# Two layers of sliding-window attention and MLP: a list scheduler's order, q and k projected token-major and transposed by DMA

## The chip, the core and the metric

The kernel runs on one core of a Trainium2 chip. The metric is the device time of one launch in microseconds (us). Engines are named PE (TensorE), ACT (ScalarE), DVE (VectorE), POOL (GpSimd) and SP (SyncE, which here only issues DMAs). Each engine works through its own list of instructions in order and waits on semaphores for the others.

## What is computed

Sequence 2048, width D = 576, 32 heads of 18, a causal window of 256, MLP width F = 4608. Two layers with the same weights, each an attention block and an MLP block with residuals:

```python
def _A_ref(x, wqkv, wo):            # H = 32, Dh = 18, W = 256
    qkv = (x @ wqkv).reshape(B, S, 3, H, Dh)...
    scores = einsum("bhqd,bhkd->bhqk", q, k) * Dh ** -0.5
    mask = (i - j >= 0) & (i - j < W)
    p = softmax(where(mask, scores, -1e9))
    return einsum("bhqk,bhkd->bhqd", p, v)... @ wo
def _B_ref(x, w1, b1, w2, b2):
    y = _layernorm(x)
    return gelu(y @ w1 + b1) @ w2 + b2
x = x + _A_ref(_layernorm(x), wqkv, wo)
x = x + _B_ref(_layernorm(x), w1, b1, w2, b2)   # and both once more
```

Inputs and output are bfloat16.

## The kernel before

**Tiles and chunks.** The sequence is 16 tiles of 128 tokens; four tiles make a chunk, so two layers are eight chunks (`NK`). x stays in SBUF as float32 (`x_res`). Everything for a chunk k: layer norm (`ln_stats` on DVE at L280 and L282, `ln_rstd` on ACT as exp of a logarithm at L286 and L288, the normalise on DVE at L299), a transpose by DMA from SP (L302) to `xnTa` or `xnTm`; projections to q, k, v; attention; out-projection; layer norm again; MLP.

**Projections.** `qk_piece` (L329) computes q and k feature-major: the stationary operand is a slice of weights spread to 32 columns per head (`wq_pad`, `wk_pad`, built at the start by `scat`), the moving one is `xnTa` with 512 token columns; five matmuls for four heads, evicted at L335 or L337 directly into `qT` and `kT`. `v_piece` (L356) is token-major: `xnTa` stationary, 288 columns of `wv_sb` moving. `kT` is a ring of six tiles, `vA` one of ten; `qT` has one buffer.

**Attention.** Eight groups of four heads, three units each. `scores` (L388) writes PSUM banks 0 to 3, ACT takes the exponentials into `pT` (L396, two instructions), POOL masks (L407), `pv` (L426) accumulates in bank 4, DVE divides into `attq`. `att_T` transposes `attq` by DMA (L446), `outproj` (L464) and `resid` (L454) add to x.

**MLP.** In two halves of 18 slices of F. `mm1` (L479): five matmuls of 512 columns per slice into banks 0 to 3, gelu on ACT into `hT` (L483; one buffer for both halves). `mm2_piece` (L491): 288-column matmuls over the slices into banks 5 and 6, then `resid`. Weights are loaded by DMA from SP for every chunk anew (`w1_load` L309, `w2_load` L316). At L666 POOL adds the bias b2 to x.

**Order.** `Sched` (L36 on) records a list per engine in the order of the calls and inserts waits. The order is written by hand in the loop at L614. Iteration k, with km = k - 1: normalise for chunk k+1; `G_part(km, 0)` is mm1 of the first half; `E_part(k, 0)` is heads 0 to 3 of chunk k with mm2 of that half and q and k pieces of chunk k+1 as fillers between the units; `G_part(km, 1)`; `E_part(k, 1)` with the second half's mm2; then the tail: `att_T`, the last q and k pieces, `outproj` with statistics and normalise to `xnTm`, v pieces and the last mm2 tile between, and the w2 loads. The next iteration begins with mm1, which reads that `xnTm`. Iteration 8 has only the MLP of the last chunk. ACT loads the gelu table before and the exp table after each `G_part`.

Of the kernel before, what the change touches and what calls it, by code (L numbers as in the profile page):

```python
# [7 lines left out]
P = 128  # L8
# [148 lines left out]

def build_kernel(nc, A_x, A_wqkv, A_wo, B_x, B_w1, B_b1, B_w2, B_b2, out):
    S_ = 2048
# [5 lines left out]
    G = 8  # L165
    NT = S_ // P
# [5 lines left out]
    DHALF = 288  # L172
    CT = 4
    NCH = NT // CT
    CW = CT * P
    NK = NL * NCH
# [4 lines left out]
    NB1 = 4  # L181

    S = Sched(nc)

# [4 lines left out]
    w1_sb = sb("w1_sb", [P, NB1, KD, 512], BF16)  # L189
# [5 lines left out]
    xnTa = sb("xnTa", [P, KD, CW], BF16)  # L195
    xnTm = sb("xnTm", [P, KD, CW], BF16)
    qT = sb("qT", [P, G, CW], BF16)
# [3 lines left out]
    attq = sb("attq", [P, CT, KD * 128], BF16)  # L201
    attT = sb("attT", [P, KD, CW], BF16)
    hT = sb("hT", [P, NFH, 512], BF16)
    NXN = 4
# [5 lines left out]
    lnv = sb("lnv", [P, NT], FP32)  # L210
    rstd = sb("rstd", [P, NT], FP32)
    rinv = sb("rinv", [P, 2, 16], FP32)
# [3 lines left out]
    def bank(i):  # L216
        return ps[:, i * 512:(i + 1) * 512]
# [3 lines left out]
    B_X = 7  # L221
# [501 lines left out]
```

## Time and profile before

| | us |
|---|---|
| median of 3 runs | 1178.65 (1178.14 to 1182.75) |
| the profiled execution, its own time | 1179.94 |
| its span, first to last instruction | 1178.2 |
| PE busy | 1028.5 |
| ACT busy | 654.1 |
| POOL busy | 353.2 |
| DVE busy | 306.8 |
| mean granted PE clock, share of 2.4 GHz | 0.961 |

The rows below come from one profiled execution. A start is counted from the first instruction. Matmuls overlap in their pipeline, so the duration of one matmul is longer than its share of the time; what a matmul costs in a sequence is read from the distance of two starts.

### The profile page before, as it was taken

What the parts mean: (1) busy time and instruction counts of PE and PEld (TensorE: products, weight loads), DVE (VectorE), ACT (ScalarE), POOL (GpSimd) and SP (SyncE); (2) the same over time, 40 slices, a digit from 0 to 9 for tenths busy, and PEclk for the clock granted to TensorE, in tenths of its full rate; (3) what the DMA queues carried; (4) which work ended last, traced back from release to release, by engine and by line L of the source; (5) the groups of instructions that cost most, each with busy time, mean ns of one, the idle gap of its engine ahead of it and who ended that gap; (6) DMA issues with size and microseconds to landing.
All of it is one profiled execution on the core that took longest, in us unless ns stands there. A gap on an engine that the chain in (4) does not pass through costs nothing.

```text
span 1178.2 us, 22128 instructions
## 1 busy us (share of the span) xinstructions
PE 1028.5 (87%) x9312; PEld 580.0 (49%) x9312; DVE 306.8 (26%) x615; ACT 654.1 (56%) x927; POOL 353.2 (30%) x429
## 2 busy tenths in 40 slices
PE   3677799979999799898999899997998979898798
PEld 1233354544645445455545546454454644545366
DVE  8432312251213412034021521115020240102111
ACT  3364466646657276663656456573756627674432
POOL 9253132330414304151132314143040521424100
PEclk9897899999999899999999999999999989998899
DMA  9501414117230363306332171312633025331640
GB/s 242 155 2 23 85 41 140 54 34 205 70 103 22 71 169 91 101 2 147 92 112 81 29 191 61 112 51 50 199 92 101 17 52 169 93 105 35 179 130 21
DMA packets 158562, 109.78 MB, mean 93 GB/s; under 512 B 74176, under 2 KB 157760, under 8 KB 158464
## 3 DMA queue, kind: packets, MB, share of 16 engines
q1 hardware_dynamic: 151872, 105.41, 32.6%
q0 software_dynamic: 4768, 0.31, 0.8%
q10 hardware_dynamic: 1824, 2.65, 0.6%
q8 instruction: 73, 1.20, 0.4%
q14 instruction: 25, 0.20, 0.1%
HBM read 90.10 MB, written 2.36 MB: 78 GB/s over the span
## 4 chain that ended last, share of the span: by engine, by line
PE 73%; DVE 10%; ACT 8%; issue 5%; POOL 3%; DMA 1%; SPq 0%; POOLq 0%; DVEq 0%
PE ps L479 27%; PE ps L491 21%; PE ps L329 10%; ACT pT L396 5%; PE ps L426 5%; PE ps L388 5%; PE ps L356 4%; DVE st_all L280 3%; DVE x_res L454 3%; POOL pT L407 2%; DVE xn L299 2%; PE ps L464 1%; ACT hT L483 1%; ACT vA L365 1%; DVE mv_all L282 1%
## 5 line engine op out<-in xcount | busy, mean ns | idle before, releaser
L407 POOL TENSOR_SCALAR_AFFINE_SELECT pT<-pT 128x512 bf16<-128x512 bf16 (+1 forms) x368 | 277.4, 776 | 633.2 <-ACT pT L396 622.2
L396 ACT ACTIVATE pT<-ps 128x1024 bf16<-128x1024 f32 (+2 forms) x384 | 351.7, 967 | 168.7 <-PE ps L388 168.5
L479 PE MATMUL ps<-xnTm,w_sb 128*128 128x512 bf16 x1440 | 323.6, 387 | 6.0 <-DMA xnTm<-xn 6.0
L491 PE MATMUL ps<-w_sb,hT 128*128 128x288 bf16 x2304 | 317.5, 290 | 8.7 <-DVE x_res L454 8.1
L483 ACT ACTIVATE hT<-ps,b1col 128x512 bf16<-128x512 f32 x288 | 195.6, 687 | 138.9 <-PE ps L479 138.8
L491 PEld LDWEIGHTS ps<-w_sb,hT 128*128 128x128 bf16 x2304 | 218.6, 99 | 76.7 <-DVE x_res L454 11.3
L479 PEld LDWEIGHTS ps<-xnTm,w_sb 128*128 128x128 bf16 x1440 | 142.8, 100 | 180.8 <-issue 19.8
L454 DVE TENSOR_TENSOR x_res<-ps,x_res 128x576 f32<-128x576 f32 x80 | 60.0, 750 | 370.8 <-PE ps L491 321.9
L426 PE MATMUL ps<-vA,pT 128*128 128x20 bf16 x2880 | 102.8, 172 | 21.1 <-POOL pT L407 20.6
L426 PEld LDWEIGHTS ps<-vA,pT 128*128 128x128 bf16 x2880 | 85.7, 96 | 59.2 <-issue 41.6
L388 PE MATMUL ps<-qT,kT 32*128 32x384 bf16 (+2 forms) x1408 | 74.6, 279 | 37.2 <-ACT pT L396 25.5
L356 PE MATMUL ps<-wv_sb,xnTa 128*128 128x288 bf16 x320 | 58.6, 325 | 49.5 <-ACT vA L365 29.2
L329 PE MATMUL ps<-xnTa,wk_pad 128*128 128x512 bf16 x320 | 86.9, 406 | 16.3 <-DVE kT L335 6.3
L329 PE MATMUL ps<-xnTa,wq_pad 128*128 128x512 bf16 x320 | 84.7, 398 | 5.6 <-DVE kT L335 5.0
L335 DVE CAST qT<-ps 128x512 bf16<-128x512 f32 x49 | 33.8, 690 | 208.6 <-PE ps L329 208.4
L666 POOL TENSOR_TENSOR x_res<-x_res,b2bc 128x576 f32<-128x576 f32 x32 | 44.8, 1400 | 109.5 <-DVE xn L299 109.5
L388 PEld LDWEIGHTS ps<-qT,kT 32*128 32x128 bf16 x1408 | 22.3, 92 | 101.6 <-ACT pT L396 61.5
L356 PEld LDWEIGHTS ps<-wv_sb,xnTa 128*128 128x128 bf16 x320 | 31.5, 108 | 71.3 <-ACT vA L365 37.6
L365 ACT ACTIVATE vA<-ps 128x288 bf16<-128x288 f32 x64 | 26.1, 408 | 65.2 <-PE ps L356 65.2
L335 DVE CAST kT<-ps 128x256 bf16<-128x256 f32 (+1 forms) x78 | 40.4, 541 | 61.7 <-PE ps L329 61.7
L329 PEld LDWEIGHTS ps<-xnTa,wk_pad 128*128 128x128 bf16 x320 | 28.6, 102 | 54.5 <-ACT qT L337 9.4
L286 ACT ACTIVATE lnv<-mv_all 128x1 f32<-128x1 f32 x64 | 12.6, 197 | 68.7 <-DVE mv_all L282 68.7
(35 smaller groups left out, 383.9 us busy)
## 6 DMA issues: line engine op xcount, KB each, us to landing
w_sb<-in_B_w_dram SPq DMA_DIRECT2D x144, 288.0 KB, 4.6
w_sb<-in_B_w_dram SPq DMA_DIRECT2D x72, 512.0 KB, 4.0
w_sb<-in_B_w_dram SPq DMA_DIRECT2D x72, 64.0 KB, 3.8
hT<-in_A_x_dram SPq DMA_DIRECT2D x4, 576.0 KB, 10.8
out_dram<-xn SPq DMA_DIRECT2D x16, 144.0 KB, 1.8
w_sb<-in_A_wqkv_dram ACTq DMA_DIRECT2D x1, 1152.0 KB, 7.7
wv_sb<-in_A_wqkv_dram ACTq DMA_DIRECT2D x1, 576.0 KB, 10.5
wo_sb<-in_A_wo_dram ACTq DMA_DIRECT2D x1, 576.0 KB, 12.7
```

The lines of the kernel that those rows point to most:

```text
L329: ins = e.matmul(bank(bnk)[:, 0:CW], wpad[:, c, g * 128:(g + 1) * 128], xnTa[:, c, :], start=(c == 0), stop=(c == KD - 1))
L335: S.add("dve", lambda e: e.tensor_copy(dst, src), reads=[f"pb{bnk}"], writes=wr)
L356: ins = e.matmul(bank(bnk)[:, 0:DHALF], xnTa[:, c, i * 128:(i + 1) * 128], wv_sb[:, c, hh * DHALF:(hh + 1) * DHALF], start=(c == 0), stop= ...
L388: ins = e.matmul(psS[:, j, col:col + nq * 128], kT[32 * j:32 * j + 32, g, s, :], qT[32 * j:32 * j + 32, g, qo * 128:(qo + nq) * 128], star ...
L396: S.add("act", lambda e, h2=h2: e.activation(pT[:, sl, 2 * h2:2 * h2 + 2, lo:hi], psS[:, 2 * h2:2 * h2 + 2, lo:hi], ACT.Exp, scale=SCALE), ...
L407: S.add("pool", lambda e, ap=ap, pat=pat, sgn=sgn, kind=kind: e.affine_select(ap, ap, pattern=pat, compare_op=(ALU.is_ge if kind == "d" el ...
L426: ins = e.matmul(bank(B_O)[:, o:o + VW], pT[:, sl, j, col + qi * 128:col + (qi + 1) * 128], vA[:, sv, 4 * g + j, :], start=(first and n == ...
L454: S.add("dve", lambda e: e.tensor_tensor(dst, src, xr, ALU.add), reads=[f"pb{b0}", f"pb{b0 + stp}", f"x{t}"], writes=[f"x{t}" if outp is N ...
L479: ins = e.matmul(bank(bnk)[:, 0:CW], w1_sb[:, sl, c, fo * 128:(fo + 1) * 128], xnTm[:, c, :], start=(c == 0), stop=(c == KD - 1))
L483: S.add("act", lambda e: e.activation(hT[:, fl, :], bank(bnk)[:, 0:CW], ACT.Gelu_apprx_tanh, bias=b1col[:, f:f + 1]), reads=[f"pb{bnk}", " ...
L491: ins = e.matmul(bank(bb[0] + hh * bb[1])[:, 0:DHALF], hT[:, fl, i * 128:(i + 1) * 128], w2_sb[:, fl, hh * DHALF:(hh + 1) * DHALF], start= ...
L666: S.add("pool", lambda e, t=t: e.tensor_tensor(x_res[:, t, :], x_res[:, t, :], b2bc[:, :], ALU.add), reads=[f"x{t}", "b2"], writes=[f"x{t}"])
```

## The change

A task class and a list scheduler (`Task`, `Plan`, `Bank`) come between the code and `Sched`. Each operation is given a planned duration, a latency and a priority; `Plan.schedule` takes again and again the task that can start earliest, among equals the one with the lowest priority number, and so fixes each engine's order once, when the program is built. PSUM banks 5, 6 and 7 are given out by it to projections, out-projections and mm2, one bank per half row of 288 columns; before, they had fixed places. `PAIR` is False, so its branches are not built.

q and k are projected like v, token-major, with 288 moving columns, evicted by DVE with 32 columns per head into `qn` (six buffers, zeroed once by POOL), and moved to `qT` and `kT` by DMA transposes of 128x1024, one for each tile and each of q and k, issued from SP. `wq_pad`, `wk_pad` and the spreading of weights go. `xnTm` has two buffers. v is evicted by DVE instead of ACT. `resid` works on halves of 288 columns, and mm2 does one half of the columns after the other, in pieces of six slices.

rstd is computed by POOL, a multiply-add and a power with exponent -0.5, for one tile or four at once, in place of ACT's logarithm and exponential. The exp table is another set.

The loop orders, by priority: heads 0 to 3 of chunk k with the second mm2 half of chunk k-2, mm1 of the first half of k-1, heads 4 to 7 of k with mm2 of that half, the projections of k+1 and the tail of k, then mm1 of the second half of k-1. Its mm2 comes in the next iteration. At the start the first chunk's x is loaded alone, the rest of x after the k weights, and w1 and w2 after the transposes of the first chunk.

```diff
+    def schedule(self):
...
+        while len(order) < n:
+            best = None
+            for e in ENGS:
+                for t in released[e]:
+                    st = max(free[e], t.ready)
+                    if t.alloc:
+                        fb = sorted(bank_free.values())
+                        if len(fb) < len(t.alloc):
+                            continue
+                        st = max(st, fb[len(t.alloc) - 1])
+                    key = (round(st, 3), t.prio, t.idx)
+                    if best is None or key < best[0]:
+                        best = (key, t, st)
...
+        for st, t in order:
...
+                self.S.add(t.eng, t.fn, [nm(r) for r in t.reads], [nm(w) for w in t.writes], dma=t.dma, ring=t.ring)
...
-    wq_pad = sb("wq_pad", [P, KD, G * 128], BF16)
-    wk_pad = sb("wk_pad", [P, KD, G * 128], BF16)
-    wv_sb = sb("wv_sb", [P, KD, D], BF16)
+    wqkv = sb("wqkv", [P, KD, 3 * D], BF16)
...
+    xnTm = sb("xnTm", [P, 2, KD, 512], BF16)
...
+    qn = sb("qn", [P, NQN, H * 32], BF16)
...
+    for i in range(NQN):
+        add("pool", lambda e, i=i: e.memset(qn[:, i, :], 0.0), writes=[f"qn{i}h{h}" for h in range(2)], cost=1.0, prio=-9)
...
-        S.add("act", lambda e: e.activation(lnv[:, t:t + 1], mv_all[:, t, 1:2], ACT.Ln, bias=bias, scale=scale),
-              reads=[f"mv{t}"], writes=[f"lnv{t}"])
-        S.add("act", lambda e: e.activation(rstd[:, t:t + 1], lnv[:, t:t + 1], ACT.Exp, scale=-0.5),
-              reads=[f"lnv{t}"], writes=[f"rstd{t}"])
...
+        add("pool", lambda e: e.tensor_scalar(vtmp[:, t0:t0 + n], var, sc, bi, op0=ALU.mult, op1=ALU.add),
+            reads=mvs, writes=[f"vt{t}" for t in ts], cost=0.15, prio=prio)
+        add("pool", lambda e: e.tensor_tensor(rstd[:, t0:t0 + n], vtmp[:, t0:t0 + n], nhalf[:, 0:n], ALU.pow),
+            reads=[f"vt{t}" for t in ts] + ["nhalf"], writes=rds, cost=0.4, prio=prio)
...
+    def qkv(k, i, prio):
+        l, t0, nt = CH[k]
+        A = l * NT + t0 + i
+        for n, w in enumerate("qkv"):
+            dest = [f"v{A % VS}h{o}" for o in range(2)] if w == "v" else [f"qn{qn_ctr[0] % NQN}h{o}" for o in range(2)]
+            bs = two_out(lambda o, c, r: xnTa[r, c, i * 128:(i + 1) * 128],
+                         lambda o, c, r, n=n: wqkv[r, c, n * D + o * HB:n * D + (o + 1) * HB], HB,
+                         [f"w{w}A", f"w{w}B", f"w{w}C", f"xa{i}"], prio + 0.01 * n, after=dest)
...
+                    add("dve", lambda e, o=o, b=bs[o], qv=qv: e.tensor_copy(qv[:, o * 16:(o + 1) * 16, 0:DH],
+                                                                          bank(b)[:, 0:HB].rearrange("p (h d) -> p h d", d=DH)),
+                        reads=[bs[o]], writes=[f"qn{sl}h{o}"], cost=0.42, prio=prio)
+                if w == "q":
+                    dst, dn = qT[:, :, i * 128:(i + 1) * 128], f"q{i}"
+                else:
+                    dst, dn = kT[:, :, A % KS, :], f"k{A % KS}"
+                add("sp", lambda e, dst=dst, sl=sl: e.dma_start_transpose(dst, qn[:, sl, :]),
+                    reads=[f"qn{sl}h0", f"qn{sl}h1"], writes=[dn], dma="t", ring=8, cost=2.1, lat=1.6, prio=prio)
...
     for k in range(NK + 1):
...
+        b = 4 * k
+        last = k == NK
+        if not last:
+            if 0 < k < NK - 1:
+                ln1(k + 1, b + 1)
+            E(k, range(0, 4), b - 0.5)
+        if k >= 2:
+            mm2(k - 2, 1, b)
+            w2_load(0, b + 1)
+        if k >= 1:
+            G_part(k - 1, 0, b + 1)
+        if not last:
+            E(k, range(4, 8), b + 1.5)
+        if k >= 1:
+            mm2(k - 1, 0, b + 2)
+            w2_load(1, b + 3)
+        if not last:
+            if k + 1 < NK:
+                for i in range(CH[k + 1][2]):
+                    qkv(k + 1, i, b + 2.2 + 0.2 * i)
+            tail(k, b + 1.9)
+        if k >= 1:
+            G_part(k - 1, 1, b + 3)
+    mm2(NK - 1, 1, b + 4)
+    PL.schedule()
```

## Rows read from the trace of the kernel before

**Rows 1.** The page's busy times: engine, us, share of the span, instructions.
```profile
PE 1028.5 (87%) x9312; PEld 580.0 (49%) x9312; DVE 306.8 (26%) x615; ACT 654.1 (56%) x927; POOL 353.2 (30%) x429
```

**Rows 2.** The page's chain of work that ended last, by engine.
```profile
PE 73%; DVE 10%; ACT 8%; issue 5%; POOL 3%; DMA 1%; SPq 0%; POOLq 0%; DVEq 0%
```

**Rows 3.** PE's timeline at mm1: start, length (us), line, operation, count, [idle before].
```profile
132.44 20.51 PE L479 MATMUL ps<-xnTm,w_sb 128*128 128x512 bf16 x90
...
970.84 19.59 PE L479 MATMUL ps<-xnTm,w_sb 128*128 128x512 bf16 x90
...
1097.72 22.51 PE L479 MATMUL ps<-xnTm,w_sb 128*128 128x512 bf16 x90 [6.02 <-DMA xnTm<-xn]
```

**Rows 4.** Windows of one iteration: length, busy (instructions), clock, DMA share, GB/s.
```profile
828.58:848.17 19.59, 19.59 (x92) 8.68 (x89) 2.05 (x4) 14.17 (x27) 0.00 (x0) 1.00 0.97 274
848.17:888.18 40.01, 35.13 (x463) 22.43 (x463) 9.51 (x19) 26.51 (x27) 18.41 (x24) 1.00 0.26 79
888.18:909.45 21.27, 21.27 (x96) 9.15 (x92) 0.71 (x2) 11.68 (x17) 0.00 (x0) 0.92 0.38 112
909.45:946.60 37.15, 33.34 (x440) 20.30 (x441) 10.73 (x23) 25.23 (x26) 18.41 (x24) 1.00 0.10 29
946.60:968.30 21.70, 17.54 (x109) 11.07 (x107) 10.05 (x21) 4.82 (x16) 5.61 (x4) 0.84 0.31 61
```

**Rows 5.** PE's timeline, work back to back.
```profile
46.66 1.24 PE L329 MATMUL ps<-xnTa,wq_pad 128*128 128x512 bf16 x5
47.74 1.24 PE L329 MATMUL ps<-xnTa,wk_pad 128*128 128x512 bf16 x5
...
848.95 0.40 PE L388 MATMUL ps<-qT,kT 32*128 32x384 bf16 x8 [0.78 <-ACT hT L483]
849.28 2.38 PE L491 MATMUL ps<-w_sb,hT 128*128 128x288 bf16 x18
...
858.40 0.56 PE L426 MATMUL ps<-vA,pT 128*128 128x20 bf16 x16
858.82 2.37 PE L491 MATMUL ps<-w_sb,hT 128*128 128x288 bf16 x18
861.11 0.40 PE L388 MATMUL ps<-qT,kT 32*128 32x384 bf16 x8
...
951.05 0.79 PE L356 MATMUL ps<-wv_sb,xnTa 128*128 128x288 bf16 x5
951.67 3.84 PE L464 MATMUL ps<-wo_sb,attT 128*128 128x288 bf16 x30
```

**Rows 6.** Groups by shape: count, busy us, mean ns, idle before and its releaser.
```profile
L396 ACT ACTIVATE pT<-ps 128x1024 bf16<-128x1024 f32 x320 | 310.1, 1021 | 145.3 <-PE ps L388 145.2
L396 ACT ACTIVATE pT<-ps 128x768 bf16<-128x768 f32 x32 | 24.2, 807 | 15.3 <-PE ps L388 15.3
L396 ACT ACTIVATE pT<-ps 128x512 bf16<-128x512 f32 x32 | 17.4, 594 | 8.0 <-PE ps L388 8.0
L335 DVE CAST kT<-ps 128x256 bf16<-128x256 f32 x42 | 15.8, 417 | 20.2 <-PE ps L329 20.2
L407 POOL TENSOR_SCALAR_AFFINE_SELECT pT<-pT 128x512 bf16<-128x512 bf16 x256 | 159.4, 635 | 538.0 <-ACT pT L396 527.8 <-PE ps L329 7.2 <-PE ps L491 3.0
```

**Rows 7.** PE's timeline, two score units of the first chunk, three units apart.
```profile
69.81 0.29 PE L388 MATMUL ps<-qT,kT 32*128 32x256 bf16 x4 [0.44 <-ACT pT L396]
75.69 0.29 PE L388 MATMUL ps<-qT,kT 32*128 32x256 bf16 x4 [0.44 <-ACT pT L396]
```

**Rows 8.** The line of the transposes: SP's ns min/median/max, and us to landing.
```profile
L302 SPq DMA_TRANSPOSE xnTa<-xn x32: 1199/1218/2325, 11.8 to 838.4; - x32
DMA to landing us min/median/max: 2.5/2.6/6.1
```

**Rows 9.** PE's timeline at the start.
```profile
17.50 4.67 PE L356 MATMUL ps<-wv_sb,xnTa 128*128 128x288 bf16 x20 [17.50 <-DMA xnTa<-xn]
51.07 0.34 PE L388 MATMUL ps<-qT,kT 32*128 32x384 bf16 x4
```

More of the change, by code (lines that the diff above doesn't have):

```diff
@@ L155, in _, with __init__ @@
             run_engine("sp", sp)
+class Task:
+    __slots__ = ("idx", "eng", "fn", "reads", "writes", "cost", "lat", "prio", "dma", "ring", "handles", "alloc",
+                 "npred", "succ", "ready", "end", "plain")
+    def __init__(self, **kw):
+        for k, v in kw.items():
+            setattr(self, k, v)
+        self.npred = 0
+        self.succ = []
+        self.ready = 0.0
+        self.end = None
+class Bank:
+    def __init__(self):
+        self.no = None
+        self.left = 0
+        self.free = 0.0
@@ L181, in build_kernel @@
     NB1 = 4
+    NXN = 4
+    NQN = 6
+    TOPF = D - 512
+    CH = [(l, t, 4) for l in range(NL) for t in range(0, NT, 4)]
+    NK = len(CH)
     S = Sched(nc)
+    PL = Plan(S, [5, 6, 7])
+    add = PL.add
     def sb(name, shape, dtype):
@@ L426, in fn @@
                         ins = e.matmul(bank(B_O)[:, o:o + VW], pT[:, sl, j, col + qi * 128:col + (qi + 1) * 128],
-                                       vA[:, sv, 4 * g + j, :], start=(first and n == 0), stop=(last and n == tot - 1),
+                                       vA[:, (T0 + so) % VS, 4 * g + j, :], start=(first and n == 0), stop=(last and n == tot - 1),
                                        skip_group_check=True)
@@ new lines, in pv, with E @@
+            add("dve", lambda e: e.tensor_tensor(dst, O4, rb, ALU.mult), reads=[f"pb{B_O}", f"ri{r}"], writes=[f"aq{g}"], cost=0.46,
+                prio=prio)
+    def E(k, gs, prio):
+        us = units_of(k)
+        pend = []
+        for g in gs:
+            for n, parts in enumerate(us):
+                sl = scores(k, g, parts, prio)
+                pend.append((g, parts, sl, n == 0, n == len(us) - 1))
+                if len(pend) > 2:
+                    pv(k, *pend.pop(0), prio - 0.1)
+        for p in pend:
+            pv(k, *p, prio - 0.1)
@@ L594, in build_kernel @@
-    S.add("pool", lambda e: e.memset(lnv[:, 0:1], 0.0), reads=xbar, writes=[f"h{f}" for f in range(NFH)] + ["lnv0"])
-    def ln1(k):
-        for i in range(CT):
-            t = (k % NCH) * CT + i
-            ln_rstd(t, False)
-            ln_norm_T(t, xnTa, "xa")
-    w1n = [NB1]
-    def G_part(k, hf, banks):
-        table("gelu")
-        for n, f in enumerate(range(hf * NFH, (hf + 1) * NFH)):
-            mm1(k, hf, f, banks[n % len(banks)])
-            if f % 4 == 3 and w1n[0] < NK * 9:
-                w1_load(w1n[0])
-                w1n[0] += 1
-        table("exp")
@@ new lines, in table, with ln1 @@
+            fn = lambda e: e.preload_act_table(ACT.Gelu_apprx_tanh)
+        add("act", fn, cost=1.3, lat=0.0, fifo="act", plain=True, prio=prio)
+    def ln1(k, prio):
+        l, t0, nt = CH[k]
+        ts = list(range(t0, t0 + nt))
+        ln_rstd(ts, False, prio)
+        for i, t in enumerate(ts):
+            ln_norm_T(t, i, xnTa, "xa", prio)
+    table("exp", -10)
+    for t in range(n0):
+        ln_stats(t, -6, x_in, f"xin{t}")
+    for i in range(n0):
+        ln_rstd([i], False, -20)
+        ln_norm_T(i, i, xnTa, "xa", -6, x_in, f"xin{i}")
```

700 lines of the change are left out of this document (360 added, 340 removed).

## The prediction

> **What bounds the kernel now.** I read the busy line first [rows 1]: TensorE is busy for 1028.5 us of 1178.2, ScalarE for 654.1, VectorE for 306.8, GpSimd for 353.2. The chain of work that ended last agrees, with 73% of the span on PE [rows 2]. So two things can shorten the kernel: less PE work, and fewer of the 150 us in which PE does nothing or runs at the lower clock.
>
> The timeline of PE then cuts the span at the up-projections (mm1) of the MLP's first halves [rows 3]. The first starts at 132.4 us, the seventh at 970.8: six iterations of 139.7 us. The seventh takes 126.9, and the last MLP 80.5. The windows of one iteration [rows 4] show where the 139.7 go: mm1 19.6, heads 0 to 3 with mm2 40.0, mm1 again 21.3 (clock 0.92), heads 4 to 7 37.2, and then 21.7 of projections, with a clock of 0.84 and 17.5 busy.
>
> What that work costs back to back is read as differences of starts [rows 5]: a unit of scores 0.33 us, its PV product 0.42, eighteen mm2 matmuls 2.29 (0.127 each), a q or k piece of five 512-column matmuls 1.08, a v piece of five 288-column ones 0.62 (0.124 each), thirty out-projections 3.84 (0.128). One iteration's work is then mm1 39.2 + mm2 288 x 0.127 = 36.6 + 24 units x 0.75 = 18.0 + q and k 16 x 1.08 = 17.3 + v 8 x 0.62 = 5.0 + out 5.1 = 121.2. It takes 139.7, so the order written by hand loses **18.5 us per iteration**.
>
> **The change part by part.** *q and k token-major.* Their 640 matmuls have 288 columns in place of 512: 16 x 1.08 us become 80 x 0.124 = 9.9 in an iteration, 7.4 less, and 59 over the kernel. That lies on the path, since PE is the bound. Work of an iteration: **113.8 us**.
>
> VectorE gets 192 evictions of 128x288 in place of its casts; the nearest row is 417 ns for 128x256 [rows 6]. At 0.44 that is 84 us against some 75 removed; ScalarE loses its share of the evictions and the rstd steps, and has only more slack. The residual adds go by halves, some 10 us more. VectorE stays near 330 us, a third of the span.
>
> *The transposes by DMA.* 64 transposes of 128x1024 join SP's queue. The trace has only 128x640: 1.20 us of SP each, up to 2.33, landing 2.6 us after issue, at worst 6.1 [rows 8]. I scale by width, 1.6 x 1.2 = 1.92 us, between 1.2 (no growth) and 3.7 (the slowest scaled). q has one buffer and k's ring of six tiles overlaps the chunk before, so all eight of a chunk wait until the last scores of the previous chunk are read. From there SP issues 8 x 1.92 = 15.4 us, four attT and four xnTm transposes (9.6), and some 3 of w1 loads, all in one queue, and lands 1.4 later: the next chunk's heads can run about **30 us** after the last scores. Meanwhile PE has the rest of the fillers and the up-projection before those heads, 10 + 19.6. It just covers; each further microsecond costs one per iteration. The w2 loads wait for the last mm2 tile and stand behind the transposes.
>
> By the Trainium skill's "DMA: Bandwidth & Descriptors", section "Latency and other measured facts", a DMA transpose moves 261 GB/s; the 160 KB in 1.20 us here are 137 GB/s. By the page a q or k transpose would take 1.0 us, and the one place where they stand bare (the start, below) would be 7 us shorter.
>
> *The shift by half a cycle.* Before, an iteration ends in a chain: last PV, attT, out-projection, statistics, rstd, normalise, xnTm, then mm1 at once. After, another mm1 half and four heads lie between; xnTm has two buffers for that. The 21.7 us stretch at the low clock goes, and late things there (rstd among them) have some 50 us of cover.
>
> *The list scheduler.* mm1 and scores still share PSUM banks 0 to 3 and ScalarE, so half a chunk's heads and half an MLP alternate as before. Three units without filler in the way take 5.88 us, of which ScalarE's exponentials are 4.84 [rows 7, 6]: 0.35 us of hand-over per unit. A full unit is 2 x 1.02 + 0.35 = 2.39, and with a filler's piece sometimes in front 2.6: 31.5 us for twelve. The chain through banks 0 to 3 is 2 x (31.5 + 0.8 + 19.6) = 104, the 0.8 being the wait for the last gelu [rows 5]. PE's 113.8 are more, and q, k and v of the next chunk may now fill either half. So PE stays the bound. I add 6 for late masks, evictions and transposes: **120 per iteration**, between 115 (PE alone) and 128.
>
> *rstd by Pool pow.* 86 small GpSimd instructions in place of 128 on ScalarE. No row shows a pow; a mask of 128x512 takes 635 ns [rows 6], so I take 0.3 us each, between 0.1 and 1.4. Queued behind them on GpSimd are masks, and behind those PV: at most 8 x 1.4 = 11 us per iteration on an engine with 60% idle. On VectorE a normalise that waits for rstd holds the evictions behind it, and those hold the three spare banks and so PE's fillers: up to 2 us for each of five such waits in an iteration where a pair of masks goes first, 10 us. That and GpSimd's own delay are in the 128 above. At the start, without cover, it is about 1 us.
>
> *The start.* The first projection waits until 17.5, the first scores until 51.1 [rows 9]. Only the first x tiles load first now, nothing is scattered into padded weights, and GpSimd has shorter memsets. What that gives no row tells; between 17.5 and half of it I stay near the row and take the first projection at 14, the chunk's 120 matmuls 20 us with the first half at the low clock (twenty took 4.67 [rows 9]), last transpose 3 later: scores at 37. Chunk 0's heads have no MLP to fill and take 8 x 5.88 + 2 = 49: to 86. Then the eight transposes stand bare, about 20 us: 106. Four heads of chunk 1 now come before the first mm1: 28. First mm1 at **134**, between 120 and 145. In that stretch PE can already do three tiles of chunk 2's q, k, v, 11 us, which the first iteration then lacks.
>
> *The end.* The seventh iteration has no next chunk: 19.6 + 32.5 + 19.6 + 5 = 77. The last stage has one mm2 half more, because of the shift: 3 x 18.3 (144 matmuls at 0.127) + 2 x 19.6 + 3 of hand-overs = 97, where 80.5 were.
>
> **Sum**: 134 + (6 x 120 - 11) + 77 + 97 = 1017 us. The profiled execution has 1179.94 us for a span of 1178.2, the median is 1178.65; with 1 us outside the span I forecast **1018 us**.
>
> **The rivals.** *A. The planned order does not hold on the chip.* Each engine's order is fixed from planned durations, and where a real one is longer the engines wait in order, as now. If as much is lost as by hand, an iteration is 113.8 + 18.5 = 132: 1018 + 6 x 12 = 1090. For it: the losses now are many waits under 1 us. Against it: fillers cover them, and three banks serve all fillers.
>
> *B. Transposes late by some.* If SP's 30 us become 41, each of the seven boundaries costs 11: 1018 + 77 = 1095. For it: the largest SP time of 2.33. Against it: the median is 1.2.
>
> *C. Slower than before.* The place is SP's queue between two chunks. If every 128x640 transpose takes 2.33 there and each wide one 3.7, the stretch grows by 8 x 1.8 + 8 x 1.1 = 23 us; seven times that is 161, which gives 1179. Any landing like the 6.1 on top makes it slower, about 1200. It decides from 23 us per boundary.
>
> *D. PE without a gap.* 115 per iteration and a start at 120: 1018 - 30 - 14 = 974. For it: the scheduler has fillers from two chunks. Against it: only three spare banks.
>
> *E. No gain that shows*: A and B together, 1018 + 72 + 77 = 1167, with a little more the old time.
>
> **How the numbers follow.** The forecast (985 to 1055) gets 0.55, A 0.13, B 0.11, D 0.12, C 0.06, E 0.03. A, B and D are faster: 0.91. The range reaches to D and past B: 968 to 1100; C and E stay out. About 0.5% is what a measurement of this kernel can tell from no change; within that I put 0.03, slower 0.06.
>
> **What would show it.** q and k matmuls of 288 columns at about 0.124 us; PE busy near 960; mm1 starts of successive first halves 120 apart; a granted clock near 1.0 in every stretch after the first mm1; SP times of about 1.9 us for the wide transposes, and no PE idle longer than a few us that ends on qT or kT after the start. The forecast is wrong if the scores wait for transposes at each chunk, if PE's idle falls by less than 60 us, or if the first mm1 is far from 134.

## The result and the profile after

| | before | after |
|---|---|---|
| median, us (4 runs each) | 1178.39 (1175.69 to 1182.75) | 1035.97 (1033.63 to 1036.42) |
| ratio, 95% interval | | 0.8784 (0.8754 to 0.8814) |
| the profiled execution, its own time | 1179.94 | 1036.42 |
| its span | 1178.2 | 1034.6 |
| first mm1 starts at | 132.4 | 141.3 |
| an iteration, mean of six | 139.7 | 118.8 |
| the seventh | 126.9 | 103.0 |
| from the last first-half mm1 to the end | 80.5 | 77.3 |
| mean granted PE clock | 0.961 | 0.939 |

The time lies 18 us over the forecast of 1018 and inside its range. The span is 143.6 us shorter: 8.9 lost before the first mm1, 125.4 gained in the six iterations, 23.9 in the seventh, 3.2 at the end.

The page of after, its busy times and the shares of its chain of work that ended last; they answer to [rows 1] and [rows 2]:

```profile
PE 942.6 (91%) x9312; PEld 585.8 (57%) x9312; DVE 317.0 (31%) x771; ACT 591.9 (57%) x705; POOL 380.3 (37%) x519
...
PE 81%; POOL 5%; issue 5%; DMA 4%; ACT 2%; DVE 2%; SPq 1%; POOLq 0%; DVEq 0%
```

PE is busy 85.9 us less, and idle for 92.0 us where it was 149.7: 57.7 less. VectorE's 10% of the chain before are 2% now: the end of an iteration with its statistics and normalises is off the path.

Windows of after: the stretch from chunk 0's first scores to chunk 1's, the one from there to the first mm1, and then the iteration from 735.3 in four parts (mm1, heads 4 to 7, mm1, heads 0 to 3); columns as in [rows 4], with which the last four compare:

```profile
33.76:98.90 65.14, 37.99 (x537) 23.84 (x536) 25.19 (x69) 36.29 (x48) 32.47 (x46) 0.68 0.50 114
98.90:141.29 42.39, 31.20 (x399) 20.65 (x398) 23.62 (x56) 22.49 (x24) 26.61 (x34) 0.81 0.31 61
735.32:755.31 19.99, 19.99 (x114) 9.35 (x112) 0.97 (x3) 12.80 (x18) 1.11 (x2) 1.00 0.33 101
755.31:791.16 35.85, 32.86 (x452) 22.69 (x450) 8.92 (x21) 24.37 (x26) 17.23 (x22) 0.94 0.41 101
791.16:819.25 28.09, 27.79 (x158) 14.43 (x159) 11.30 (x28) 13.83 (x19) 9.91 (x14) 0.95 0.88 181
819.25:854.31 35.06, 28.01 (x401) 19.13 (x400) 5.81 (x14) 24.46 (x26) 17.23 (x22) 0.87 0.37 116
```

The fifth part of before, 21.7 us at a clock of 0.84, is gone. What PE did there now lies inside the second mm1, which takes 28.1 us in place of 21.3, or among the heads. In the last part fillers (PE work that stands between the units and covers their waits) are short: PE is busy for 28.0 of 35.1 us and the granted clock is 0.87, a mix of the two levels of 1.2 and 2.4 GHz (1.00 is the upper one, 0.50 the lower); in the first stretch, with PE busy for 38.0 of 65.1 us, it is 0.68. Why they are short in this iteration, the sixth, is seen in the groups of PE's projections before 141.29 (first two lines) and in the iteration from 735.32 (last two):

```profile
L485 PE MATMUL ps<-wqkv,xnTa 128*128 128x288 bf16 x272 | 48.7, 312 | 20.4 <-DMA xnTa<-xn 20.4
L491 PE MATMUL ps<-wqkv,xnTa 128*128 128x288 bf16 x68 | 21.1, 310 | 0.0
...
L485 PE MATMUL ps<-wqkv,xnTa 128*128 128x288 bf16 x36 | 6.2, 303 | 0.0
L491 PE MATMUL ps<-wqkv,xnTa 128*128 128x288 bf16 x9 | 2.7, 304 | 0.0
```

A chunk has 120 projections. 340 run ahead of the first mm1, so 100 of chunk 2 are done early, and the sixth iteration has 45 left of its own 120.

PE's waits in after (us in total, times, longest):

```profile
PE ps L601 <- POOL pT L584: 28.2, 29, 3.1
PE ps L554 <- ACT pT L563: 27.4, 33, 2.1
PE ps L485 <- DMA xnTa<-xn: 20.4, 3, 14.8
PE ps L680 <- ACT pT L563: 5.6, 8, 1.2
PE ps L485 <- DMA attT<-attq: 5.4, 9, 1.9
PE ps L554 <- DMA qT<-qn: 1.0, 1, 1.0
```

The exponentials and masks of the attention lead. The transposes of q and k cost PE 1.0 us in all.

### The profile page after: what moved, and what is told of

Same layout as the page of the kernel before. It is cut to its first block, busy times and chain, and to the rows that moved or that the text cites. A ratio compares the mean times of both kernels' runs of the same rounds, so it can differ in the third digit from the quotient of the medians.

```text
span 1034.6 us, 22287 instructions
## 1 busy us (share of the span) xinstructions
PE 942.6 (91%) x9312; PEld 585.8 (57%) x9312; DVE 317.0 (31%) x771; ACT 591.9 (57%) x705; POOL 380.3 (37%) x519
## 4 chain that ended last, share of the span: by engine, by line
PE 81%; POOL 5%; issue 5%; DMA 4%; ACT 2%; DVE 2%; SPq 1%; POOLq 0%; DVEq 0%
PE ps L716 28%; PE ps L680 24%; PE ps L485 10%; PE ps L687 6%; PE ps L601 5%; PE ps L554 5%; POOL pT L584 5%; PE ps L491 2%; DMA attT<-attq 2%; ACT pT L563 2%; DMA xnTa<-xn 2%; DVE st_all L413 1%; DMA hT<-in_A_x_dram 0%; SPq L365 0%; POOL rstd L426 0%
## 5 line engine op out<-in xcount | busy, mean ns | idle before, releaser
L680 PE MATMUL ps<-xnTm,w_sb 128*128 128x512 bf16 x1152 | 305.8, 389 | 5.6 <-ACT pT L563 5.6
L716 PEld LDWEIGHTS ps<-w_sb,hT 128*128 128x128 bf16 x2304 | 212.0, 97 | 70.3 <-issue 17.9
L635 DVE TENSOR_TENSOR x_res<-ps,x_res 128x288 f32<-128x288 f32 x160 | 71.0, 451 | 350.5 <-PE ps L716 308.8
L485 PE MATMUL ps<-wqkv,xnTa 128*128 128x288 bf16 x768 | 130.9, 301 | 20.4 <-DMA xnTa<-xn 20.4
L601 PEld LDWEIGHTS ps<-vA,pT 128*128 128x128 bf16 x2880 | 97.3, 98 | 56.0 <-POOL pT L584 38.1
L601 PE MATMUL ps<-vA,pT 128*128 128x20 bf16 x2880 | 102.1, 173 | 28.6 <-POOL pT L584 28.2
L687 PE MATMUL ps<-xnTm,w_sb 128*128 128x512 bf16 x288 | 111.8, 388 | 0.0
L554 PE MATMUL ps<-qT,kT 32*128 32x384 bf16 (+2 forms) x1408 | 79.2, 294 | 28.6 <-ACT pT L563 27.4
L485 PEld LDWEIGHTS ps<-wqkv,xnTa 128*128 128x128 bf16 x768 | 70.8, 101 | 50.0 <-issue 22.9
L521 DVE CAST qn<-ps 128x288 bf16<-128x288 f32 x128 | 58.1, 456 | 69.4 <-PE ps L491 46.8
L611 DVE RECIPROCAL rinv<-ps 128x16 f32<-128x16 f32 x64 | 16.5, 257 | 143.2 <-PE ps L601 143.0
L491 PE MATMUL ps<-wqkv,xnTa 128*128 128x288 bf16 x192 | 57.6, 300 | 0.0
L436 DVE TENSOR_SCALAR xn<-x_res,mv_all,rstd 128x576 bf16<-128x576 f32 x60 | 42.8, 724 | 39.4 <-DMA xnTm<-xn 25.4
L424 POOL TENSOR_SCALAR vtmp<-mv_all 128x1 f32<-128x1 f32 (+1 forms) x43 | 9.3, 216 | 105.4 <-DVE mv_all L415 103.1
```

The lines of the kernel that those rows point to most:

```text
L485: ins = e.matmul(bank(bs[o])[:, 0:n], lhs(o, c, full), rhs(o, c, full), start=(c == 0), stop=False)
L491: ins = e.matmul(bank(bs[o])[:, 0:n], lhs(o, 4, full), rhs(o, 4, full), start=False, stop=True)
L521: add("dve", lambda e, o=o, b=bs[o], qv=qv: e.tensor_copy(qv[:, o * 16:(o + 1) * 16, 0:DH], bank(b)[:, 0:HB].rearrange("p (h d) -> p h d", ...
L554: ins = e.matmul(psS[:, j, col:col + nq * 128], kT[32 * j:32 * j + 32, g, (T0 + so) % KS, :], qT[32 * j:32 * j + 32, g, qo * 128:(qo + nq) ...
L601: ins = e.matmul(bank(B_O)[:, o:o + VW], pT[:, sl, j, col + qi * 128:col + (qi + 1) * 128], vA[:, (T0 + so) % VS, 4 * g + j, :], start=(fi ...
L635: add("dve", lambda e: e.tensor_tensor(x_res[:, t, sl], bank(b)[:, 0:HB], x_res[:, t, sl], ALU.add), reads=[b], writes=[f"x{t}h{hh}"], cos ...
```

## The experiments

Three questions: which part of the change brings the gain, what bounds an iteration now, and how thin the cover of the transposes is. Stage times are starts of first-half mm1s in PE's timeline: first mm1 | mean of six iterations | the seventh. After has 141.3 | 118.8 | 103.0. Ratios are to the kernel before on the same chip, with 95% intervals. The runs were on several chips, on which the kernel before has medians of 1174.6 to 1182.2 us; where two runs differ by less than 1% in microseconds, the ratios are to be compared.

### Which part brings the gain

**The columns alone, in the order of before.** Kernel before, q and k matmuls with 288 columns' worth of work.

```diff
-    n = CW
+    n = CW if c == 0 else 232
```

> The kernel before with q and k pieces of 512 + 4 x 232 = 1440 moving columns in place of 2560, as many as the change has for the same tokens (token columns 232 to 511 get one of five parts of the sum: computation left out). The hand order and all else stay. If each of these pieces lies on PE's path, 128 pieces x (1.08 - 0.61) = 60 us go: 1119, between 1110 and 1130. If the hand order gives them back as waits, because these pieces are the fillers under which ScalarE's exponentials run: above 1143.

Measured: 1170.23 us, ratio 0.9946 (0.9928 to 0.9964). Of some 60 us of PE work 7 show. The busy times here, and PE's wait for the exponentials in before and here (us in total, times, longest):

```profile
PE 999.4 (85%) x9312; PEld 592.0 (51%) x9312; DVE 305.5 (26%) x615; ACT 654.3 (56%) x927; POOL 353.2 (30%) x429
```
```profile
PE ps L388 <- ACT pT L396: 25.5, 43, 2.0
```
```profile
PE ps L389 <- ACT pT L397: 40.4, 71, 2.5
```

PE is busy for 29.1 us less, not 60: the mean granted clock is 0.918 where it was 0.961, and matmuls that the edit leaves alone take longer (one of v 360 ns in the mean, 325 in before). And PE is idle for 21.3 us more (171.0 against 149.7), 14.9 of it at this wait. The fillers became shorter, PE waits for the exponentials instead, and half of the saved work comes back at the lower clock. Less PE work is worth almost nothing in the order written by hand.

**The list scheduler without the shift.** After, with the loop of before: mm1 of the first half, heads 0 to 3 with its mm2, mm1 of the second half, heads 4 to 7 with its mm2, then projections and tail.

```diff
+        if k >= 1:
+            G_part(k - 1, 0, b)
         if not last:
-            E(k, range(0, 4), b - 0.5)
+            E(k, range(0, 4), b + 0.5)
         if k >= 1:
-            G_part(k - 1, 0, b + 1)
+            mm2(k - 1, 0, b + 1)
+            w2_load(1, b + 2)
+            G_part(k - 1, 1, b + 2)
...
+            E(k, range(4, 8), b + 2.5)
...
+            mm2(k - 1, 1, b + 3)
```

> The changed kernel without the shift by half a cycle: the loop order of before (first mm1 half, heads 0 to 3 with its mm2, second mm1 half, heads 4 to 7 with its mm2, projections and tail, then at once the next mm1), ordered by the same list scheduler. If the shift is what hides the tail's chain (last PV, attT, out-projection, normalise, xnTm: some 17 us, with some 12 us of filler left), about 5 us per iteration come back, less what the start gains: 1056, between 1043 and 1075. If the scheduler with its fillers covers the tail by itself: 1036 within 6 or lower. If the shift carries all that the hand order lost (18.5 us per iteration): above 1090.

Measured: 1152.62 us, ratio 0.9807 (0.9779 to 0.9836); 122.4 | 135.9 | 137.9. The third expectation came true. Scheduler, columns and transposes together bring 2%; the shift is worth some 117 us. The window of this kernel's stretch between two MLPs, its part after the last mm2 matmul, and PE's first mm1 after it:

```profile
742.00:802.20 60.20, 40.53 (x492) 27.06 (x492) 21.12 (x48) 26.50 (x27) 27.46 (x36) 0.80 0.53 124
```
```profile
764.99:802.20 37.21, 17.54 (x197) 10.60 (x198) 16.49 (x37) 10.97 (x11) 17.65 (x24) 0.67 0.76 169
```
```profile
802.24 1.49 PE L680 MATMUL ps<-xnTm,w_sb 128*128 128x512 bf16 x3 [10.02 <-DMA xnTm<-xn]
```

mm1 waits 10.0 us for the tail's `xnTm`, six times over (59.9 us in 6). Ahead of that the mm2 matmuls are used up after seven of the stretch's twelve units, and the other five and the tail leave PE busy for 17.5 of 37.2 us, at a clock of 0.67. That is the chain that the prediction read in [rows 4], and the list scheduler doesn't hide it with this loop.

**rstd on ScalarE, in the shifted order.**

```diff
-        add("pool", lambda e: e.tensor_scalar(vtmp[:, t0:t0 + n], var, sc, bi, op0=ALU.mult, op1=ALU.add),
...
-        add("pool", lambda e: e.tensor_tensor(rstd[:, t0:t0 + n], vtmp[:, t0:t0 + n], nhalf[:, 0:n], ALU.pow),
...
+        add("act", lambda e: e.activation(vtmp[:, t0:t0 + n], var, ACT.Ln, bias=bi, scale=sc),
...
+        add("act", lambda e: e.activation(rstd[:, t0:t0 + n], vtmp[:, t0:t0 + n], ACT.Exp, scale=-0.5),
...
-            fn = lambda e: e.preload_act_table_set("exp_and_others")
+            fn = lambda e: e.preload_act_table_set("natural_log_exp_and_others")
```

(In this kernel, the next one and the one with each transpose planned twice, `resid`'s second half also counts as a writer of the tile's buffer `xn`, one more wait that their orders need.)

> The changed kernel with rstd again by logarithm and exponential on ScalarE, in place of GpSimd's power, and the exp table set of before. If rstd is off the path, as the prediction says: 1036 within 6. If ScalarE's queue, in which it now waits between exponentials, delays the normalise and with it PE: 1046 or more. If GpSimd's power (0.6 us for one tile, 1.0 for four) costs something in the changed kernel: 1028 or less.

Measured: 1125.97 us, ratio 0.9583 (0.9559 to 0.9608); 150.7 | 131.0 | 112.5. Putting 86 small instructions back on ScalarE costs 90 us. Its timeline between the heads and the second mm1, and PE's line that waits for it:

```profile
207.17 1.94 ACT L563 ACTIVATE pT<-ps 128x1024 bf16<-128x1024 f32 x2 [1.56 <-PE ps L554]
223.27 0.20 ACT L424 ACTIVATE vtmp<-mv_all 128x1 f32<-128x1 f32 x1 [14.16 <-DVE mv_all L415]
...
229.45 0.20 ACT L426 ACTIVATE rstd<-vtmp 128x1 f32<-128x1 f32 x1
229.67 1.28 ACT L732 ACT_TABLE_LOAD   x1
230.97 2.42 ACT L695 ACTIVATE hT<-ps,b1col 128x512 bf16<-128x512 f32 x4
```
```profile
232.11 1.49 PE L680 MATMUL ps<-xnTm,w_sb 128*128 128x512 bf16 x3 [6.43 <-ACT hT L695]
```

The logarithms stand in ScalarE's list after the last exponentials and before the gelu table. They wait 14.2 us for the statistics of the tail, so every gelu waits too; mm1's banks stay full, and PE stops after the work in front of it.

**rstd on ScalarE, without the shift.** Both edits above together.

> The changed kernel without the shift and with rstd on ScalarE. In this order the tail's layer norm falls into the stretch in which ScalarE has the exp table. If rstd on ScalarE cost 90 us in the shifted order because there it falls between heads and gelu and holds the gelu table back, it costs nothing here: 1153 within 12. If it costs by its place in ScalarE's queue as such: 1153 + 60 or more.

Measured: 1139.85 us, ratio 0.9635 (0.9610 to 0.9660), even 13 us below the same loop with Pool's power (1152.62, ratio 0.9807). So the power by itself brings nothing. It is what lets the shift work: only there does the tail's layer norm meet the gelus of another MLP on ScalarE. With the power the shift is worth 117 us, with rstd on ScalarE 14 (1139.85 to 1125.97). What the additional wait for `xn` costs in the shifted order was not run by itself; in this loop, which has it too, no loss is seen.

### What bounds an iteration now

**More PE work.** q and k matmuls with 512 moving columns, planned at their length.

```diff
+            wid = HB if w == "v" else 512
-                         lambda o, c, r, n=n: wqkv[r, c, n * D + o * HB:n * D + (o + 1) * HB], HB,
+                         lambda o, c, r, n=n, wid=wid: wqkv[r, c, n * D + o * HB:n * D + o * HB + wid], wid,
```

> The changed kernel with q and k projected over 512 moving columns in place of 288 (224 columns too many, which nobody reads), the planned durations of these matmuls to match, all else as it is. If PE's work is the bound in the new order and the saved columns lie on the path, the 640 matmuls cost 640 x (0.216 - 0.122) = 60 us more: 1036 + 60 = 1096, between 1085 and 1105. If the chain through banks 0 to 3 or SP's queue sets the time and PE has slack, most of it is hidden: below 1055.

Measured: 1062.31 us, ratio 0.9044 (0.9018 to 0.9070); 152.8 | 121.0 | 103.5. Of the 59 us of the prediction's first term, 26 come back: 11.5 before the first mm1, and 2.2 per iteration where PE got 7.4 more to do. (This kernel has a planned order of its own.)

**Less PE work, in after's order.** Four of the five matmuls of a q or k piece with 64 columns.

```diff
+                    m = 64 if thin and c else n
-                    ins = e.matmul(bank(bs[o])[:, 0:n], lhs(o, c, full), rhs(o, c, full), start=(c == 0), stop=False)
+                    ins = e.matmul(bank(bs[o])[:, 0:m], lhs(o, c, full), rhs(o, c, full)[:, 0:m], start=(c == 0), stop=False)
```

> The changed kernel with q and k pieces of 288 + 4 x 64 = 544 moving columns in place of 1440 (columns 64 to 287 get one of five parts of the sum: computation left out), in the planned order of the changed kernel, unchanged. PE has 128 x 4 x 224 / 2400 = 48 us less to do, 6 in an iteration. If the changed kernel's iteration (119) is set by the chain through banks 0 to 3 and ScalarE, with PE's work a few us below it, little is won: 1036 down to no less than 1020. If PE's work sets it: 990. Read with the run of wide q and k, of whose 60 us only 26 came out: there PE's work (121.2 per iteration) is the bound.

Measured: 1024.49 us, ratio 0.8667 (0.8650 to 0.8684); 134.4 | 118.0 | 103.6. In its timeline such a piece takes 0.24 us where after's takes 0.62: 128 x 0.38 = 49 us less PE work. 11.5 of them show, 7 before the first mm1; in an iteration six go and 0.8 show. PE's busy time falls by 3.7 of these six in the mean (114.4 to 110.7): the clock is lower here too, 0.928 in the mean against 0.939.

The fourth iteration in windows, of the wide kernel, of after and of the thinned kernel, with 1137 recorded matmuls each (length, then PE's busy time):

```profile
514.10:636.40 122.30, 121.53 (x1137) 72.94 (x1146) 41.58 (x100) 71.41 (x90) 42.28 (x57) 1.00 0.50 119
```
```profile
500.04:615.57 115.53, 113.87 (x1137) 72.33 (x1134) 41.05 (x100) 71.04 (x89) 41.92 (x58) 1.00 0.51 126
```
```profile
490.40:605.00 114.60, 108.39 (x1137) 67.69 (x1134) 39.82 (x99) 70.32 (x88) 41.48 (x57) 1.00 0.53 129
```

7.7 us more of PE work cost 6.8; 5.5 less bring 0.9. In this iteration, with 135 projections and fewer scores than most, PE is the bound of after, but only just: the next bound lies within 1 us. In the mean of six, where others lack fillers, that next bound is already in charge at 118.8, and PE's work, 113.8 by the prediction's sum, becomes the bound once 7.4 are added: 121.2, and 121.0 were measured. What remains at 118 when PE's work shrinks is, by PE's waits, the exchange of units between PE and ScalarE through banks 0 to 3: those for masks and exponentials, 28.2 and 27.4 us in after, are 40.2 and 31.0 in the thinned kernel.

**Planned durations as measured.** Costs of exponentials, gelu, evictions, powers and transposes set to what after's trace has; below those of a power, of a q or k transpose and of a gelu.

```diff
-            reads=[f"vt{t}" for t in ts] + ["nhalf"], writes=rds, cost=0.4, prio=prio)
+            reads=[f"vt{t}" for t in ts] + ["nhalf"], writes=rds, cost=0.6 if n == 1 else 1.02, prio=prio)
...
-                    reads=[f"qn{sl}h0", f"qn{sl}h1"], writes=[dn], dma="t", ring=8, cost=2.1, lat=1.6, prio=prio)
+                    reads=[f"qn{sl}h0", f"qn{sl}h1"], writes=[dn], dma="t", ring=8, cost=1.3, lat=3.0, prio=prio)
...
-                    reads=[f"pb{bks[o]}", "b1"], writes=[f"h{fl}"], cost=0.2 + n * 0.00087, lat=0.2, fifo="act", prio=prio)
+                    reads=[f"pb{bks[o]}", "b1"], writes=[f"h{fl}"], cost=0.687, lat=0.2, fifo="act", prio=prio)
```

> The changed kernel with the planned durations of ScalarE, VectorE, GpSimd's power and the transposes set to what its trace shows (exponentials 0.05 us more each, gelu 0.687, evictions 0.456, wide transposes 1.3 on SP and 3.0 to landing); only the orders differ. If the planned order holds well enough on the chip: 1036 within 8. If the plan's errors make engines wait in order (rival A in small): 1020 or less. If any change of order costs, because the order at hand was picked among several: above 1046.

Measured: 1046.81 us, ratio 0.8894 (0.8848 to 0.8941); 138.7 | 120.8 | 103.7. The order changed, the start gained 2.6 and each iteration lost 2. What the plan has wrong about durations isn't where time is lost; the greedy choice moved the time by 1% on small changes of its input. So of a run with a planned order of its own, 1% by itself says little about its edit.

**Scores in two steps.** A unit's four heads were one task that needs banks 0 to 3 at once; here it is two, with two banks each.

```diff
-        add("pe", fn, reads=rd, writes=[f"pb{j}" for j in range(4)], cost=0.06 + ncol * 0.00053, prio=prio, lat=0.15)
+        for h2 in range(2):
+            add("pe", lambda e, js=(2 * h2, 2 * h2 + 1): fn(e, js), reads=rd, writes=[f"pb{j}" for j in (2 * h2, 2 * h2 + 1)],
+                cost=0.04 + ncol * 0.00045, prio=prio, lat=0.15)
```

> The changed kernel with a unit's scores as two tasks of two heads, so that the scores of banks 0 and 1 can run while ScalarE still takes the exponentials of banks 2 and 3. Each half pairs two heads in PE instead of four, some 0.1 us more PE per unit, 2.4 per iteration; the hand-over of 0.35 us per unit goes from the chain, 8 per iteration. If the chain is the bound: an iteration of about 116, 1036 - 20 = 1016. If PE is the bound: 1036 + 17 = 1053.

Measured: 1035.31 us, ratio 0.8754 (0.8732 to 0.8776); 130.6 | 120.8 | 98.1. Its busy times and the two waits that led in after:

```profile
PE 966.6 (94%) x9312; PEld 600.1 (58%) x9312; DVE 311.1 (30%) x771; ACT 595.7 (58%) x705; POOL 379.0 (37%) x519
```
```profile
PE ps L554 <- ACT pT L565: 6.1, 13, 1.2
PE ps L603 <- POOL pT L586: 5.0, 4, 3.1
```

The waits fell from 27.4 and 28.2 us to 6.1 and 5.0, and PE's busy time rose by 24.0, or 0.125 for each of the 192 units; its waits for `attT` rose from 5.4 to 19.1 as well. Start and seventh, where fillers are short, gain 10.7 and 4.9; the iterations, where PE is nearly full, lose 2.0 each. The sum is no difference, between the two expectations.

**In two steps only where fillers are short.** Chunks 0, 1 and 7.

```diff
+        ends = k in (0, 1, NK - 1)
+        for js in (((0, 1), (2, 3)) if ends else ((0, 1, 2, 3),)):
```

> The changed kernel with a unit's scores as two tasks of two heads in the chunks 0, 1 and 7 alone, where PE has little filler, and four heads at once in the others. In the run with all units split the first mm1 came 11 us earlier, the first iteration was 10 us shorter and the seventh 5 us, and the others gave it back to PE's added work. If the hand-over between scores and exponentials is the bound only where fillers are short: 1036 - 20 to 25 = 1011 to 1016. If splitting gains nothing by itself and the run with all units split came out even by other orders: 1030 or more.

Measured: 1008.47 us, ratio 0.8571 (0.8550 to 0.8591); 130.2 | 116.9 | 97.8. It is the fastest of all kernels here, 27.5 us below after, 2.4% by the ratios. The gain lies where units were split: 11.1 us before the first mm1, 5.8 in the first iteration and 5.3 in the sixth, which have heads of chunks 1 and 7, and 5.2 in the seventh; the four iterations between gain 0.7 in all. PE is 94% busy and the clock is 0.969:

```profile
PE 946.9 (94%) x9312; PEld 588.2 (58%) x9312; DVE 317.9 (32%) x771; ACT 593.2 (59%) x705; POOL 380.2 (38%) x519
```

### How thin the cover of the transposes is

**Each q and k transpose twice, and planned so.**

```diff
+                for _ in range(2):
+                    add("sp", lambda e, dst=dst, sl=sl: e.dma_start_transpose(dst, qn[:, sl, :]),
...
```

> The changed kernel with each transpose of q and k issued twice, to the same place, planned as two. SP's time per chunk grows by 8 x 1.3 = 10 us, between the last scores of a chunk and the first of the next. If the transposes are covered with about 5 us to spare (a wide one takes 1.3 us of SP, not the 1.92 of the prediction): 5 us at each of seven boundaries, 1036 + 35 = 1071, between 1055 and 1085. If the cover is much wider: below 1044. If each microsecond already costs one per boundary: 1036 + 73 = 1109 or more.

Measured: 1130.72 us, ratio 0.9621 (0.9589 to 0.9652); 167.6 | 130.8 | 102.2. 64 more transposes of 1.30 us of SP in the median, 83 us, cost 95. SP's own time isn't all of it: both of a pair write the same tile, so `Sched` lets the second wait until the first has landed. Here the plan puts other work between most pairs, and 23.6 us of such waits are left.

**Twice, in after's order.** The first of each two is planned at no cost; PE, ScalarE, GpSimd and VectorE have the same lists as in after.

```diff
+                for cost, lat in ((0.0, 0.0), (2.1, 1.6)):
...
+                        reads=[f"qn{sl}h0", f"qn{sl}h1"], writes=[dn], dma="t", ring=8, cost=cost, lat=lat, prio=prio)
```

> The changed kernel with each transpose of q and k issued twice, but planned at no cost, so that PE, ScalarE, GpSimd and VectorE keep the order of the changed kernel and SP only has pairs. If the 95 us of the first doubled run are SP's time on the chip (64 x 1.3 = 83): about 1120 again. If they are mostly the plan's, which put heads later and used the fillers up before them: 1036 + 7 x 5 = 1071 or less.

Measured: 1175.71 us, ratio 0.9950 (0.9926 to 0.9975); 178.6 | 135.8 | 103.5. It costs 140, 37 of it before the first mm1 and 17.0 per iteration: nearly the whole gain of the change, and more than both expectations foresaw. The load is larger than they took it: with the pairs back to back SP waits for the first landing in every one of the 64. SP's waits (us in total, times, longest):

```profile
SPq L528 <- DMA kT<-qn: 83.7, 32, 5.3
SPq L528 <- DMA qT<-qn: 65.5, 32, 5.4
```

These 149.2 us and 64 x 1.24 = 79 of issuing make SP's queue some 228 us longer, 8 x (1.24 + 2.33) = 28.6 per iteration. SP's timeline in one iteration, whose lines run over such waits, and PE's next to it:

```profile
377.92 9.42 SPq L528 DMA_TRANSPOSE qT<-qn  x4
387.43 1.12 SPq L365 DMA_DIRECT2D w_sb<-in_B_w_dram  x2
388.61 5.51 SPq L528 DMA_TRANSPOSE kT<-qn  x2
394.16 2.61 SPq L648 DMA_TRANSPOSE attT<-attq  x2
```
```profile
383.20 1.03 PE L680 MATMUL ps<-xnTm,w_sb 128*128 128x512 bf16 x4
384.07 0.38 PE L687 MATMUL ps<-xnTm,w_sb 128*128 128x512 bf16 x1
396.92 1.14 PE L485 MATMUL ps<-wo_sb,attT 128*128 128x288 bf16 x4 [12.47 <-DMA attT<-attq]
```

In the iterations it isn't the scores that wait (their 32.3 us for q and k all lie before the first mm1). The tail's `attT` transposes stand in SP's list behind those of q and k; the out-projection is fixed in the middle of mm1 on PE; so mm1 stops for 12.5 us, behind a product that doesn't concern it. Over the kernel PE waits 82.6 us in 9 there, and VectorE 66.6 us in 13 for `qn` to come free. By planning the pairs (1130.72) the scheduler takes 45 of the 140 back; SP's waits for a first landing are 23.6 us there and 149.2 here.

## The prediction, step by step

**What bounds the kernel: right, with the second bound priced too low.** PE's work per iteration is as forecast (113.8 us; after's six have 114.4 of busy time in the mean, some of it at a lower clock). The 150 us of the prediction are idle time alone; time at the lower clock counts as busy. The chain through banks 0 to 3 was put at 104 and an iteration stays at 118 when PE has less to do, as the thinned kernel shows. The windows above show the terms: the second mm1 half, taken at 19.6, is 28.1 us long (26.7 to 28.6 in all iterations), since out-projections and projections are planned into it; and twelve units, taken at 31.5 and 0.8, are 35.9 and 35.1. The 6 us that were added for late masks, evictions and transposes happened to cover this: iterations were forecast at 6 x 120 - 11 = 709 in all and took 713.0. That three tiles of chunk 2 would be projected before the first mm1 was right (100 matmuls, three tiles being 90).

**The columns: right in size.** PE's timeline of after, two pieces in a row, 0.62 us apart:

```profile
27.54 0.65 PE L485 MATMUL ps<-wqkv,xnTa 128*128 128x288 bf16 x4
...
28.16 0.65 PE L485 MATMUL ps<-wqkv,xnTa 128*128 128x288 bf16 x4
```

But "that lies on the path, since PE is the bound" failed: 7 us of 60 in the order of before, 26 in the new one. In the order of before, 31 of the 60 came back in longer matmuls at the lower clock and 21 as waits.

**The transposes: SP's time over-, landing underestimated.** After's answer to [rows 8], for the wide ones:

```profile
L528 SPq DMA_TRANSPOSE qT<-qn x32: 1231/1296/3194, 20.2 to 805.8; - x32
L528 SPq DMA_TRANSPOSE kT<-qn x32: 1232/1307/2653, 22.2 to 812.4; - x32
...
DMA to landing us min/median/max: 3.0/4.2/8.4
```

1.30 us and not 1.92 scaled by width; landing 4.2 us after issue and not 2.6. The cover held. That it is thin was about right: a microsecond more of SP per iteration was to cost one, and in after's order 28.6 more cost 17.0, through `attT`, which comes late along with q and k. Rival C had the right queue, at a load that after doesn't have, and priced it too high (161 us for 23 per boundary, where 140 were measured for 28.6); its victim was another one.

By the Trainium skill's "DMA: Bandwidth & Descriptors", section "Latency and other measured facts", a DMA transpose moves 261 GB/s where a middle dimension is not contiguous. By that figure the estimates are 1.0 us for a wide transpose and 0.63 for one of [rows 8]. SP's time was 1.30 and 1.22, so the first was nearer than my scaling by width and the second far off; and SP's time is not the transfer, which lands 3.0 us after issue at the earliest.

**The shift: right, and the largest part.** No PE wait for `xnTm` is left among the waits of after, where [rows 3] has one of 6.0. Without the shift it is 10 us per iteration, and the iteration 135.9.

**rstd by Pool power: inside its bounds, its role missed.** A power takes 0.60 us for one tile and 1.02 for four, two and three times the 0.3 that was taken between 0.1 and 1.4. The waits of VectorE's normalises for it were priced at up to 10 us per iteration; here are all of them (us in total, times, longest):

```profile
DVE xn L436 <- POOL rstd L426: 13.0, 22, 1.1
```

The step that failed is "ScalarE loses its share of the evictions and the rstd steps, and has only more slack". In the shifted order that removal is worth 90 us, since a logarithm that waits holds up the gelus behind it. The time forecast didn't suffer, because it assumed those steps gone without a price.

**The start: near by errors that cancel.** First projection at 14.8 (14 forecast) and first scores at 33.8 (37) were near. Then chunk 0's heads: 65 us where 49 was forecast. PE's timeline there:

```profile
37.20 0.47 PE L601 MATMUL ps<-vA,pT 128*128 128x20 bf16 x12 [3.10 <-POOL pT L584]
48.78 1.14 PE L485 MATMUL ps<-wqkv,xnTa 128*128 128x288 bf16 x4 [3.79 <-DMA xnTa<-xn]
...
99.94 0.61 PE L554 MATMUL ps<-qT,kT 32*128 32x384 bf16 x8 [1.01 <-DMA qT<-qn]
```

The heads were priced as if they ran alone [rows 7]. But chunk 1's projections stand among them in PE's list, one waits 3.8 us for its `xnTa`, and the scores behind it wait along; masks come late by up to 3.1; and the window's clock is 0.68. Against that the eight transposes that were to stand bare for 20 us cost 1.0: they started at 90.5, before chunk 0's last units, which don't read q's first tile. Chunk 1's first four heads took 41 where 28 was forecast, at a clock of 0.81. So 141.3 in place of 134: errors of -3, 16, -19 and 13, which leave 7; that it came near is luck. The heads' share is seen in the kernel with split scores in three chunks: chunk 1's scores start at 89.6 there, 10.4 us earlier, of the 11.1 that its first mm1 gains. So some 10 of the 16 were the exchange through one set of four banks.

**The end**: 180.3 where 77 + 97 = 174 were forecast, again with errors that cancel: the seventh took 103.0, the rest 77.3. One of the three mm2 halves put into the last stage runs ahead of its mm1 (144 matmuls, 17.8 us), and the seventh's second mm1 half is 28.2 us long, where 19.6 were taken.

**The rivals.** A, that the planned order doesn't hold, is not borne out: an iteration takes 118.8 us and not 132, and calibrating the plan doesn't help. B and C needed slower transposes than after's trace has. D, PE without a gap, isn't reached by the fastest kernel here either (1008.47, against 974).

**What was to show it.** Columns, mm1 distance and the absence of waits for qT and kT came as told. PE's busy time is 942.6 and not near 960. The clock is not near 1.0 everywhere: 0.87 in the window from 819.25, 0.939 in the mean, below the 0.961 of before. And by "wrong if PE's idle falls by less than 60 us" the forecast would have failed narrowly, with 57.7: busy time fell by more than thought and idle time by less.

**What stays open**: how much of an iteration's 118 us is the chain's own time and how much the fillers that stand in it, and what the shift would bring in an order written by hand, which wasn't tried.

## What to carry to other kernels

Parts of such a change don't add up: the columns alone brought 0.5%, scheduler, columns and transposes without the shift 2%, and the shift needs rstd off ScalarE, so test them by taking one out of the whole. Where an engine's list is fixed, ask of every operation that can wait which unrelated work stands behind it: logarithms ahead of gelus cost 90 us here for 14 of ScalarE's time, and transposes in SP's queue ahead of others stopped mm1 by way of an out-projection inside it. And use an edit that costs PE time to shorten a wait only in stages where PE has no other work: the same split of scores gave 0% everywhere and 2.4% in three chunks. When an experiment issues a thing twice, ask whether the second waits for the first: the load may be larger than the count says.

## What the chip showed that was not expected

- SP's time for a DMA transpose hardly grows with width: 1.22 us for 128x640 [rows 8], 1.30 for 128x1024. The landing does: 2.5 us against 3.0 at the least, 2.6 against 4.2 in the median; in the fuller queue of after, those of 128x640 take 2.8 to 3.5 in the median.
- A power on GpSimd has a large fixed part: 597 ns for 128x1, 1024 for 128x4.

```profile
L426 POOL TENSOR_TENSOR rstd<-vtmp,nhalf 128x1 f32<-128x1 f32 x36 | 21.5, 597 | 2.6
L426 POOL TENSOR_TENSOR rstd<-vtmp,nhalf 128x4 f32<-128x4 f32 x7 | 7.2, 1024 | 0.5
```

- The same scores in two steps of two heads raise PE's busy time by 24.0 us (942.6 to 966.6), at a higher mean clock (0.977 against 0.939).
